# Feed-forward in chunks of 384 tokens instead of 256, with a quarter of the decoded weights kept in DRAM

## The chip, the cores and the metric

One core of a Trainium2 chip runs the whole kernel. The metric is the device time of one execution in microseconds (us). A core has engines that run side by side, each with its own list of instructions: TensorE (PE, matmuls; its weight loads are shown as PEld), VectorE (DVE), ScalarE (ACT), GpSimd (POOL), and SyncE (SP), which here issues every DMA. They wait for each other on semaphores. Matmuls write PSUM, eight banks of 128 x 512 fp32; everything else lives in SBUF.

## What is computed

Attention over 8 batches, 8 heads, 576 tokens and 64 wide heads, as the sum of a pooled part (means of 4 tokens, full attention, repeated 4 times) and a local part (keys less than 4 tokens away); then a layer norm without bias, a feed-forward block with ReLU, and a residual. `moe_w_ch1` is 512 x 2048 and `moe_w_ch2` 2048 x 512, both float64, and the kernel reads them as pairs of 32-bit words.

```python
x = transpose(out_up + out_local).reshape(8, 576, 512)
mu = np.mean(x, axis=-1, keepdims=True)
var = np.mean((x - mu) ** 2, axis=-1, keepdims=True)
xn = (x - mu) / np.sqrt(var + 1e-06) * g_ln
ch = np.maximum(xn @ w_ch1, 0.0) @ w_ch2
return (x + ch).astype(np.float32)
```

## The kernel before

**Tiles and chunks.** The 8 x 576 = 4608 tokens are 36 tiles of 128. The feed-forward takes two tiles at a time: 18 chunks of 256 tokens. The 2048 inner units are 16 blocks of 128; the code handles them in 8 pairs.

**Three products for one.** Weights and activations are each split in a high and a low word of fp32r, and a product is high x low + low x high + high x high. The first product ("up", line 996) takes for a block of 128 units 12 matmuls: three terms by four pieces of the 512 inputs, with the weights as the loaded operand and 256 tokens as the moving one. The output `h` (one PSUM bank for the two blocks of a pair) goes through ACT (`hh` = ReLU rounded to fp32r, line 1003) and DVE (`hl` = the remainder, line 1007). The second product ("down", line 1019) takes `hh` and `hl`, 128 tokens by 128 units, as the loaded operand and 512 output columns of `w2` as the moving one, three matmuls a tile and block, and adds up in one PSUM bank `acc` per tile over all 16 blocks. At the end DVE adds the residual `x` (1027) and SP stores it (1033).

**Weights.** Each of the 32 keys (w1 or w2, block f) is loaded as int32 words (`s`, 347 and 352, two DMAs of 256 KB), put together by ACT (359), DVE (367, 370) and ACT (378, the high word `hi`), and DVE or POOL (383, the low word `lo`). All 64 decoded words stay in SBUF to the end.

**Norm.** A tile's `x` is the local part, copied to its rows by DMA from `xl` (659, 662), plus `up`, the pooled part, loaded from DRAM (865) and added by POOL (896). Statistics (904 to 910) and `xn` (914) follow, four transposes on PE (`px`, 923), then ACT writes `xh` (930) and DVE the remainder `xlo` (940), which the up matmuls of the chunk read.

**Rooms.** Nearly all SBUF tiles come from one pool of 88 equal units of 128 x 512 fp32, "u": raw loads, decoded weights, `xh`, `xlo`, `hh`, `hl`, `x`, `xl`, and the rest. An instruction that writes a unit waits until the last reader of what lay there is done, a DMA included.

**The order** is made by the class `Plan` (23 to 136). Every piece of work is a task with an engine, a planned duration, dependencies, a due time, the rooms that it takes and gives back, and for loads how early it may go out (`ahead`). `order()` lays the tasks out in planned time and emits them; each engine then runs its list strictly in that order, SP too. Chunks 0 and 1 are due at the same time and advance with the weights; from chunk 2 on one chunk is due every 53 planned us. Attention tasks of later batches stand between the feed-forward tasks: `ls`, `lt`, `lv` are scores, transposes and products with V of the local part (40 windows), `gq`, `gs`, `gt`, `gv` those of the pooled part.

Of the kernel before, what the change touches and what calls it, by code (L numbers as in the profile page):

```python
# [139 lines left out]
def attention_then_ffn(  # L140
# [131 lines left out]
    C1 = 5  # L272
    CHUNK = 53
    PACE = CHUNK / NPR

    def chunk_at(c):
        return T0 + (C1 * c if c < 2 else CHUNK * c)

    def pair_at(c, p):
        return chunk_at(c) + (2 * PACE if c < 2 else PACE) * p  # L280

    def norm_at(n):
        c, j = divmod(n, TPC)
        return chunk_at(c) - 6.0 + 1.0 * j
# [50 lines left out]
    weight = {}  # L335

    def weights(which, f):
# [42 lines left out]
        def low(eng):  # L380
# [24 lines left out]
    def local(i):  # L405
# [212 lines left out]
        t = add("PE", 0.75, scores_by_pair if by_pe else scores_by_block, turned, due - 6.0,  # L618
# [10 lines left out]
        for h2 in range(2):  # L629
            t = add("DVE", 0.28, lambda h2=h2: inverse(h2), (tv,), due)  # L630
# [20 lines left out]
        for e, (n, p0, r0, m, par) in enumerate(moves):  # L651

            def move(n=n, p0=p0, r0=r0, m=m, par=par):
# [7 lines left out]
                for h2 in range(2):  # L661
# [5 lines left out]
            t = add("SP", 0.76 if by_pe else 1.52, move, outs, due + 1.0, take=() if n in piece else U,  # L667
                    give=U if e == len(moves) - 1 else (), lag=LAT, kb=116)
# [58 lines left out]
    def pooled_pair(b, hg, pr, x, ready):  # L727
# [120 lines left out]
        t = add("DVE", 0.68, divided, (t,), due, take=U if b < NPB and pr == 0 else (), give=A)  # L848
# [7 lines left out]
    def norm(n):  # L856
        add = plan.add
        c, j = divmod(n, TPC)
# [66 lines left out]
        def split_hi(i):  # L925
            if j == 0:
                xh.setdefault(c, []).append(unit([P, 2, T], f"xh{c}_{i}", F32R, "xh"))
            for k in range(2):
                kc = 2 * i + k
                nc.scalar.activation(  # L930
                    xh[c][i][:, k, j * P : (j + 1) * P], pxt[n][:, kc], AF.Copy, scale=gain[:, kc : kc + 1]
                )

        def split_lo(i):
            if j == 0:
                xlo.setdefault(c, []).append(unit([P, 2, T], f"xlo{c}_{i}", F32R, "xlo"))
            ts = slice(j * P, (j + 1) * P)
            for k in range(2):
                kc = 2 * i + k
                nc.vector.scalar_tensor_tensor(  # L940
                    out=xlo[c][i][:, k, ts], in0=pxt[n][:, kc], scalar=gain[:, kc : kc + 1],
                    in1=xh[c][i][:, k, ts].bitcast(F32), op0=ALU.mult, op1=ALU.subtract,
                )

# [23 lines left out]
        t = add("DVE", 0.46, normed, (t, kept) if by_pe else (t,), due, take=U, ahead=12.0, give=A if by_pe else ())  # L968
        t = add("PE", 0.43, turn, (t,), due + 1.0, take=A, give=U, ahead=6.0)
        hi, lo = [], []  # L970
        for i in range(2):
            hi.append(add("ACT", 0.52, lambda i=i: split_hi(i), [t] + hi + his.get(c, []), due + 1.5,
                          take=() if j else rooms("xh")))
        for i in range(2):
            lo.append(add("DVE", 0.53, lambda i=i: split_lo(i), [hi[i]] + lo + xt_done.get(c, []), due + 1.5,
                          take=() if j else rooms("xlo"), give=A if i else ()))
# [4 lines left out]
    hh, hl, acc, ph = {}, {}, {}, {}  # L981
    f2_done, f1_last = {}, {}

    def ffn(c, p):
        add = plan.add
        due = pair_at(c, p)

        def up(fi):
            if fi == 0:
                ph[c, p] = psa(f"h{c}_{p}").rearrange("p (f t) -> p f t", f=2)  # L990
            f = 2 * p + fi
            wh, wl = (w.rearrange("p (c f) -> p c f", c=KC) for w in weight[1, f])
            n = 0
            for wt, xx in ((wl, xh[c]), (wh, xh[c]), (wh, xlo[c])):
                for kc in range(KC):
                    nc.tensor.matmul(  # L996
                        ph[c, p][:, fi], lhsT=wt[:, kc], rhs=xx[kc // 2][:, kc % 2], start=n == 0, stop=n == 3 * KC - 1
                    )
                    n += 1

        def relu():
            hh[c, p] = unit([P, 2, T], f"hh{c}_{p}", F32R, "hh")
            nc.scalar.activation(hh[c, p], ph[c, p], AF.Relu)  # L1003

        def rest():
            hl[c, p] = unit([P, 2, T], f"hl{c}_{p}", F32R, "hl")
            nc.vector.scalar_tensor_tensor(  # L1007
                out=hl[c, p].rearrange("p c t -> p (c t)"), in0=ph[c, p].rearrange("p c t -> p (c t)"), scalar=0.0,
# [107 lines left out]
```

## Time and profile before

| | |
|---|---|
| three runs | 1078.21, 1080.64, 1084.43 us; median 1080.64 |
| span of the profiled execution | 1080.9 us (no other time of it is recorded) |
| granted TensorE clock, mean | 0.989 |
| instructions | 23774; DMA issues 1165, all by SP |
| HBM | 82.58 MB read, 11.80 MB written |
| DMA queue share of 16 engines | 40.2% |

The page of the profile has, in this order: busy time of each engine; the span in 40 slices; DMA queues; the chain of work that ended last, with its shares by engine and by line; the costliest groups of instructions (line, engine, operation, output<-inputs, shape, count, busy time, mean duration, and the idle time of the engine just before them with what ended it); and the DMA issues. Other views are made from the same trace: PE's waits, stretches of time ("windows"), and the timeline, whose rows are start, duration, engine, line, operation, output<-input, shape, count, and in brackets the idle time before it and what ended that.

Two things about these numbers. Matmuls overlap in the array, so a row's duration is longer than the distance to the next start. And what a wait of one engine costs depends on whether another engine waits behind it.

### The profile page before, as it was taken

The page shows a single profiled execution, that of the slowest core. Times are in us where ns is not written, and L with a number is a line of the kernel's source. Part 1 is how long each engine was busy: PE and PEld are TensorE (multiplying, and loading weights), DVE is VectorE, ACT ScalarE, POOL GpSimd, SP SyncE. Part 2 cuts the span into 40 slices and gives each one's busy share as a digit, 9 for nine tenths or more (in the row PEclk, how much of TensorE's full clock was granted, in tenths as well). Part 3 has the DMA queues.
Part 4 walks back from the last instruction along what each step waited for, and adds up shares of the span by engine and source line. Part 5 has one row for each costly group of instructions (what it writes and reads, how often), then busy time and mean ns, then how long its engine had stood idle before and what let it go on. Part 6 is the DMA issues. An engine that isn't in the chain of part 4 may idle for free.

```text
span 1080.9 us, 23774 instructions
## 1 busy us (share of the span) xinstructions
PE 1040.3 (96%) x9290; PEld 933.6 (86%) x9290; DVE 511.9 (47%) x1309; ACT 312.7 (29%) x852; POOL 266.2 (25%) x285
## 2 busy tenths in 40 slices
PE   8987999989989999999999999999979999999998
PEld 8875898978879898989898989898968988888997
DVE  7699954434243535345344443645424353543211
ACT  5675633222222322132222221223212222222110
POOL 4234454314004221141213231142311400100000
PEclk9999899989999999999999999999999999999999
DMA  7798554625333443344343435252533333300000
GB/s 155 211 270 235 121 147 112 144 61 120 82 88 89 99 97 79 65 92 107 82 110 77 109 69 125 47 137 51 126 87 76 69 74 74 85 10 30 9 20 20
DMA packets 289296, 104.34 MB, mean 97 GB/s; under 512 B 237945, under 2 KB 276089, under 8 KB 289185
## 3 DMA queue, kind: packets, MB, share of 16 engines
q1 hardware_dynamic: 289185, 102.83, 40.2%
q8 instruction: 73, 1.20, 0.5%
q14 instruction: 38, 0.31, 0.1%
HBM read 82.58 MB, written 11.80 MB: 87 GB/s over the span
## 4 chain that ended last, share of the span: by engine, by line
PE 78%; DMA 9%; DVE 5%; SPq 4%; issue 2%; ACT 1%; POOL 1%; DVEq 0%; ACTq 0%; POOLq 0%
PE h L996 33%; PE acc L1019 32%; PE gv L802 3%; DMA s<-in_moe_w_ch_dram 2%; PE lv L596 2%; PE ls L540 2%; DMA x<-xl 2%; PE gs L766 2%; PE lt L575 1%; SPq L419 1%; PE px L923 1%; PE gt L785 1%; SPq L662 1%; DVE cva L370 1%; SPq L428 1%
## 5 line engine op out<-in xcount | busy, mean ns | idle before, releaser
L1019 PE MATMUL acc<-hi,hl 128*128 128x512 f32 x576 | 239.1, 415 | 10.2 <-DVE hl L1007 8.5
L1019 PE MATMUL acc<-lo,hh 128*128 128x512 f32 x576 | 228.5, 397 | 0.0
L1019 PE MATMUL acc<-hi,hh 128*128 128x512 f32 x576 | 226.8, 394 | 0.0
L1007 DVE SCALAR_TENSOR_TENSOR hl<-h,hh 128x512 fp32r<-128x512 f32 x144 | 98.9, 687 | 242.8 <-ACT hh L1003 222.8
L1003 ACT ACTIVATE hh<-h 128x512 fp32r<-128x512 f32 x144 | 86.1, 598 | 433.5 <-PE h L996 379.7
L996 PE MATMUL h<-xh,lo 128*128 128x256 f32 x1152 | 193.5, 290 | 0.0
L996 PE MATMUL h<-xlo,hi 128*128 128x256 f32 x1152 | 185.6, 284 | 0.0
L996 PE MATMUL h<-xh,hi 128*128 128x256 f32 x1152 | 185.6, 283 | 0.0
L996 PEld LDWEIGHTS h<-xh,lo 128*128 128x128 f32 x1152 | 169.4, 190 | 17.6 <-POOL lo L383 0.2
L996 PEld LDWEIGHTS h<-xlo,hi 128*128 128x128 f32 x1152 | 159.4, 192 | 0.0
L996 PEld LDWEIGHTS h<-xh,hi 128*128 128x128 f32 x1152 | 159.1, 192 | 0.0
L896 POOL TENSOR_TENSOR x<-x,up 128x512 f32<-128x512 f32 x32 | 41.2, 1289 | 376.8 <-DMA x<-xl 264.5
L1019 PEld LDWEIGHTS acc<-hi,hl 128*128 128x128 f32 x576 | 110.1, 191 | 27.5 <-DVE hl L1007 11.4
L1019 PEld LDWEIGHTS acc<-hi,hh 128*128 128x128 f32 x576 | 109.2, 190 | 25.3
L1019 PEld LDWEIGHTS acc<-lo,hh 128*128 128x128 f32 x576 | 110.3, 191 | 12.7
L930 ACT ACTIVATE xh<-px,gain 128x128 fp32r<-128x128 f32 x144 | 44.3, 367 | 79.5 <-PE px L923 43.6
L940 DVE SCALAR_TENSOR_TENSOR xlo<-px,gain,xh 128x128 fp32r<-128x128 f32 x144 | 43.0, 344 | 38.3 <-ACT xh L930 26.1
L904 DVE BATCH_NORM_STATS2 st<-x 128x6 f32<-128x512 f32 x32 | 22.1, 690 | 69.9 <-POOL x L896 68.7
L1027 DVE SCALAR_TENSOR_TENSOR x<-acc,x 128x512 f32<-128x512 f32 x36 | 24.3, 683 | 35.5 <-PE acc L1019 35.3
L546 DVE TENSOR_TENSOR ls<-ls,mask 128x256 f32<-128x256 f32 x66 | 27.0, 424 | 27.3 <-PE ls L540 22.3
L779 ACT ACTIVATE ag<-gs,gmx 96x144 f32<-96x144 f32 x96 | 28.8, 373 | 35.1 <-DVE gmx L771 33.1
L802 PEld LDWEIGHTS gv<-vd,agt 72*72 72x72 f32 x512 | 37.1, 145 | 1.5
(195 smaller groups left out, 1152.7 us busy)
## 6 DMA issues: line engine op xcount, KB each, us to landing
s<-in_moe_w_ch_dram SPq DMA_DIRECT2D x64, 256.0 KB
vwin<-in_v_dram SPq DMA_DIRECT2D x160, 64.0 KB
out_dram<-x SPq DMA_DIRECT2D x36, 256.0 KB
qr<-in_q_dram SPq DMA_DIRECT2D x264, 32.0 KB
kr<-in_k_dram SPq DMA_DIRECT2D x264, 32.0 KB
up<-ud SPq DMA_DIRECT2D x28, 256.0 KB
x<-xl SPq DMA_DIRECT2D x66, 58.0 KB
ud<-od SPq DMA_DIRECT2D x32, 72.0 KB
```

The costliest lines, as they stand in the source:

```text
L546: nc.vector.tensor_add(x.ps[n], x.ps[n], mask.unsqueeze(1).broadcast_to([P, NPAIR, 64]))
L779: nc.scalar.activation(y.a[:, c], y.ps[:, c], AF.Exp, scale=POOLED_SCALE, bias=y.mx[:, c : c + 1])
L802: nc.tensor.matmul(y.pv[:, qh, h2], lhsT=y.at[kh][:, h2, qh * GH : (qh + 1) * GH], rhs=vd[:, kh, 2 * pr + h2], start=kh == 0, stop=kh == 1,)
L896: nc.gpsimd.tensor_add(xt[n], xt[n], x.up)
L904: nc.vector.bn_stats(st, x.up if by_pe else xt[n])
L930: nc.scalar.activation(xh[c][i][:, k, j * P : (j + 1) * P], pxt[n][:, kc], AF.Copy, scale=gain[:, kc : kc + 1])
L940: nc.vector.scalar_tensor_tensor(out=xlo[c][i][:, k, ts], in0=pxt[n][:, kc], scalar=gain[:, kc : kc + 1], in1=xh[c][i][:, k, ts].bitcast(F ...
L996: nc.tensor.matmul(ph[c, p][:, fi], lhsT=wt[:, kc], rhs=xx[kc // 2][:, kc % 2], start=n == 0, stop=n == 3 * KC - 1)
L1003: nc.scalar.activation(hh[c, p], ph[c, p], AF.Relu)
L1007: nc.vector.scalar_tensor_tensor(out=hl[c, p].rearrange("p c t -> p (c t)"), in0=ph[c, p].rearrange("p c t -> p (c t)"), scalar=0.0, in1=h ...
L1019: nc.tensor.matmul(acc[c][j], lhsT=lt[:, fi, ts], rhs=rt, start=p == 0 and fi == 0 and n == 0, stop=p == NPR - 1 and fi == 1 and n == 2,)
L1027: nc.vector.scalar_tensor_tensor(out=x, in0=acc[c][j], scalar=1.0 + 2.0**-23, in1=x, op0=ALU.mult, op1=ALU.add)
```

## The change

- **Chunks.** The tiles are dealt out as 4, ten times 3, and 2: 12 chunks. Chunk 0 has 512 tokens and handles them as two parts of 256 columns; chunks 1 to 10 have 384 tokens and their up matmuls 384 columns; chunk 11 has 256.
- **Blocks one at a time.** `h` holds one block of up to 512 tokens instead of two blocks of 256. ReLU and remainder work on 128 x 384.
- **Rooms.** 88 units become 73. `xh` and `xlo` of chunks 1 to 11 get 4 buffers of their own ("xx"), high and low word of the hidden activation 2 ("hx").
- **A quarter of the weights.** For blocks 3, 7, 11 and 15 the decoded words are written to DRAM after decoding (`keep`) and their units given back after chunk 0. Every later chunk loads them anew (`again`): 4 blocks, two weights, two words, 256 KB each. Such a load may be issued up to 9 planned us before it is due, and is due 5 us before its block.
- **Plan.** Due times by tile (26 planned us each) instead of by chunk; some planned durations and lags are raised (for the DMAs from `xl` a lag of 4.0 in place of 2.5), which changes the order alone.

The core of the diff:

```diff
-    T = 256
     NT = B * S
     NTILE = NT // P
-    TPC = T // P
-    NCH = NT // T
+    TILES = [4] + [3] * ((NTILE - 4) // 3)
+    TILES += [NTILE - sum(TILES)] if sum(TILES) < NTILE else []
...
+    T = 3 * P
-    NPR = DFF // T
+    NF = DFF // P
+    KEPT = (3, 7, 11, 15)
-    NU, NSTG = 88, 2
+    NU, NSTG, NX, NHX = 73, 2, 4, 2
...
+        def keep():
+            stored[key] = dram.tile([2, P, 512], F32, tag=f"w{name}", bufs=1, name=f"w{name}")
+            for i in range(2):
+                nc.sync.dma_start(stored[key][i], weight[key][i].bitcast(F32))
...
+        if f in KEPT:
+            kept_done[key] = add("SP", 2 * DMA, keep, (t,), due + 6.0, lag=LAT, kb=512)
+        return t
+
+    def again(which, f, c, due):
+        key = (which, f)
+
+        def load():
+            words = [unit([P, 512], f"w{which}_{f}_{c}_{i}") for i in range(2)]
+            for i in range(2):
+                nc.sync.dma_start(words[i], stored[key][i])
+            weight[key] = [t.bitcast(F32R) for t in words]
+
+        return plan.add("SP", 2 * DMA, load, (kept_done[key],), due - 5.0, take=(("u", 2),), lag=LAT, kb=512, ahead=9.0)
...
+            elif j == 0:
+                to[c] = work.tile([P, KC, T], F32R, tag="xx", bufs=NX, name=f"{nm}{c}")
...
-        def up(fi):
+        def up():
+            ph[c, f] = psa(f"h{c}_{f}")
             wh, wl = (w.rearrange("p (c f) -> p c f", c=KC) for w in weight[1, f])
+            terms = [(wt, xx, kc) for wt, xx in ((wl, xh[c]), (wh, xh[c]), (wh, xlo[c])) for kc in range(KC)]
+            for part in range(2 if c == 0 else 1):
+                out = ph[c, f][:, 2 * P * part : 2 * P * (part + 1)] if c == 0 else ph[c, f][:, :tokens]
+                for n, (wt, xx, kc) in enumerate(terms):
+                    rhs = xx[:, kc, :tokens] if c else xx[2 * part + kc // 2][:, kc % 2]
+                    nc.tensor.matmul(out, lhsT=wt[:, kc], rhs=rhs, start=n == 0, stop=n == 3 * KC - 1)
 
         def relu():
-            hh[c, p] = unit([P, 2, T], f"hh{c}_{p}", F32R, "hh")
-            nc.scalar.activation(hh[c, p], ph[c, p], AF.Relu)
+            if c:
+                both = work.tile([P, 2, T], F32R, tag="hx", bufs=NHX, name=f"hx{c}_{f}")
+                hx[c, f] = [both[:, i, :tokens] for i in range(2)]
+            else:
+                hx[c, f] = [unit([P, 512], f"h{n}{c}_{f}", F32R) for n in "hl"]
+            nc.scalar.activation(hx[c, f][0], ph[c, f][:, :tokens], AF.Relu)
...
+        wide = 0.00044 * tokens if c and tokens > 2 * P else 0.12 * n_t / 2
+        t = f1_last[c] = add(
+            "PE", 12 * wide, up, xt_done[c] + [w[0], f1_last.get(c)], due, take=A,
...
```

How it moves the instructions, at three places. First PE in the steady part: a block's up matmuls followed by down matmuls. Before (rows are line, operation, output<-inputs, output shape, and x for repeats; `xh`, `xlo` are the words of the normed tokens, `hi`, `lo` those of a weight, the last number is the tile's):

```order
L996 MATMUL h_2_3637<-xh_0_3371,lo_5_1437 128x256 x2
L996 MATMUL h_2_3637<-xh_1_3404,lo_5_1437 128x256 x2
L996 MATMUL h_2_3637<-xh_0_3371,hi_5_1424 128x256 x2
L996 MATMUL h_2_3637<-xh_1_3404,hi_5_1424 128x256 x2
L996 MATMUL h_2_3637<-xlo_0_3394,hi_5_1424 128x256 x2
L996 MATMUL h_2_3637<-xlo_1_3429,hi_5_1424 128x256 x2
L1019 MATMUL acc_0_3683<-hi_0_1186,hl_0_3597 128x512
L1019 MATMUL acc_0_3683<-lo_0_1211,hh_0_3578 128x512
L1019 MATMUL acc_0_3683<-hi_0_1186,hh_0_3578 128x512
L1019 MATMUL acc_1_3684<-hi_0_1186,hl_0_3597 128x512
L1019 MATMUL acc_1_3684<-lo_0_1211,hh_0_3578 128x512
L1019 MATMUL acc_1_3684<-hi_0_1186,hh_0_3578 128x512
```

PE with the change, a block in chunk 1 whose w1 was loaded again (`w_3_1`):

```order
L1037 MATMUL h_3_3150<-xh_2807,w_3_1_1_3071 128x384 x4
L1037 MATMUL h_3_3150<-xh_2807,w_3_1_0_3070 128x384 x4
L1037 MATMUL h_3_3150<-xlo_2808,w_3_1_0_3070 128x384 x4
L1061 MATMUL acc_0_3088<-hi_2_1462,hx_2_3130 128x512
L1061 MATMUL acc_0_3088<-lo_2_1484,hx_2_3130 128x512
L1061 MATMUL acc_0_3088<-hi_2_1462,hx_2_3130 128x512
L1061 MATMUL acc_1_3089<-hi_2_1462,hx_2_3130 128x512
L1061 MATMUL acc_1_3089<-lo_2_1484,hx_2_3130 128x512
L1061 MATMUL acc_1_3089<-hi_2_1462,hx_2_3130 128x512
L1061 MATMUL acc_2_3090<-hi_2_1462,hx_2_3130 128x512
L1061 MATMUL acc_2_3090<-lo_2_1484,hx_2_3130 128x512
L1061 MATMUL acc_2_3090<-hi_2_1462,hx_2_3130 128x512
```

Twelve up matmuls now serve three tiles instead of two, and the down matmuls of a block come as nine.

Second, SP in the front, where the last two loads of w2 stand (`s_14`, `s_15`; `raw` are loads for pooling, `ud` is the pooled result on its way to DRAM). Before:

```order
L700 DMA raw3q_2133<-in_q_dram 72x4x256
L825 DMA ud_2093<-od_1_2121 72x2x128
L700 DMA raw3k_2148<-in_k_dram 72x4x256
L352 DMA s_14_0_2156<-in_moe_w_ch_dram 128x512
L352 DMA s_14_1_2157<-in_moe_w_ch_dram 128x512
L700 DMA raw3v_2187<-in_v_dram 72x4x256
L700 DMA raw3v_2204<-in_v_dram 72x4x256
L352 DMA s_15_0_2222<-in_moe_w_ch_dram 128x512
L352 DMA s_15_1_2223<-in_moe_w_ch_dram 128x512
```

SP with the change:

```order
L892 DMA up_2604<-ud_1966 128x1x512
L726 DMA raw5k_2640<-in_k_dram 72x4x256
L688 DMA x_1464<-xl_2588 58x4x64 x2
L688 DMA x_1464<-xl_2588 30x4x64 x2
L688 DMA x_2663<-xl_2588 28x4x64 x2
L359 DMA s_14_0_2712<-in_moe_w_ch_dram 128x512
L359 DMA s_14_1_2713<-in_moe_w_ch_dram 128x512
L892 DMA up_2752<-ud_1966 128x1x512
L851 DMA ud_2755<-od_0_2738 72x2x128
L359 DMA s_15_0_2762<-in_moe_w_ch_dram 128x512
L359 DMA s_15_1_2763<-in_moe_w_ch_dram 128x512
```

The loads have moved behind those of the pooled keys of the fifth half batch and behind the first moves of the local part into `x`: the load for block 15 was SP's 174th transfer and is its 235th.

Third, ACT around the `xh` of one tile and the tile after it, with the semaphores that an instruction waits for (`PE`, `DVE`, `Activation` are engines, `DMAHW0` to `DMAHW7` the DMAs). Before, tiles 26 and 27, the place at 800 to 810 us of the trace:

```order
L1003 ACTIVATE hh_5_10352<-h_5_10287 128x512 [waits PE_49]
L1003 ACTIVATE hh_6_10402<-h_6_10355 128x512 [waits PE_49]
L930 ACTIVATE xh_0_10420<-px_10404,gain 128x128 [waits PE_49,Activation_49]
L930 ACTIVATE xh_0_10420<-px_10404,gain 128x128
L930 ACTIVATE xh_1_10438<-px_10404,gain 128x128 [waits DMAHW4_49,DMAHW5_49,DMAHW1_49,DMAHW6_49,DMAHW0_49,DMAHW7_49,DVE_49,Activation_49]
L930 ACTIVATE xh_1_10438<-px_10404,gain 128x128
L930 ACTIVATE xh_0_10420<-px_10468,gain 128x128 [waits PE_49]
L930 ACTIVATE xh_0_10420<-px_10468,gain 128x128
L1003 ACTIVATE hh_7_10494<-h_7_10425 128x512 [waits DMAHW2_49,DVE_49]
```

ACT with the change, two tiles of a later chunk:

```order
L1045 ACTIVATE hx_12_6825<-h_12_6798 128x384 [waits PE_49,Activation_49]
L955 ACTIVATE xh_6870<-px_6849,gain 128x128 [waits PE_49]
L955 ACTIVATE xh_6870<-px_6849,gain 128x128
L955 ACTIVATE xh_6870<-px_6849,gain 128x128 [waits DVE_49]
L955 ACTIVATE xh_6870<-px_6849,gain 128x128
L1045 ACTIVATE hx_13_6918<-h_13_6827 128x384 [waits PE_49,Activation_49]
L955 ACTIVATE xh_6870<-px_6895,gain 128x128 [waits PE_49]
L955 ACTIVATE xh_6870<-px_6895,gain 128x128
L955 ACTIVATE xh_6870<-px_6895,gain 128x128 [waits DVE_49]
L955 ACTIVATE xh_6870<-px_6895,gain 128x128
```

`xh` and the hidden activation no longer wait for DMAs there: in the whole list of ACT 13 of 136 rows of `xh` and 46 of 144 of `hh` named a DMA before, with the change none of 128 and 2 of 192.

More of the change, by code (lines that the diff above doesn't have):

```diff
@@ L847, in pooled_pair @@
         lastg.v = lastg.vd[hg] = t
-        t = add("DVE", 0.68, divided, (t,), due, take=U if b < NPB and pr == 0 else (), give=A)
+        t = add("DVE", 0.8, divided, (t,), due, take=U if b < NPB and pr == 0 else (), give=A)
         od_done.append(t)
@@ new lines, in rest, with down @@
+                op0=ALU.max, op1=ALU.subtract,
+            )
+        def down():
+            if f == 0:
+                acc[c] = [psa(f"acc{c}_{j}") for j in range(n_t)]
+            wh, wl = weight[2, f]
+            hh, hl = hx[c, f]
+            for j in range(n_t):
+                ts = slice(j * P, (j + 1) * P)
+                for n, (lt, rt) in enumerate(((hl, wh), (hh, wl), (hh, wh))):
+                    nc.tensor.matmul(acc[c][j], lhsT=lt[:, ts], rhs=rt, start=f == 0 and n == 0, stop=last and n == 2)
@@ L1042, in ffn @@
-        f1_last[c] = ups[-1]
-        t = add("ACT", act(512), relu, ups, due, take=rooms("hh"))
-        t = add("DVE", dve(512), rest, (t,), due, take=rooms("hl"), give=A)
-        prev = f2_done.get(c)
-        for fi in range(2):
-            prev = add(
-                "PE", 1.38, lambda fi=fi: down(fi), (t, wdone[2, 2 * p + fi], prev),
-                due + (2 * PACE if c < 2 else PACE) * (OFF0 if c < 2 else 2) + 0.1 * fi,
-                take=(("a", TPC),) if p == 0 and fi == 0 else (), give=rooms("hh", "hl") if fi else (),
-            )
@@ L1052, in ffn @@
-        f2_done[c] = prev
-        if p == NPR - 1:
-            for j in range(TPC):
-                t = add("DVE", dve(512), lambda j=j: finish(j), (prev,), due + 1.5 * PACE, give=A)
-                add("SP", DMA, lambda j=j: store(j), (t,), due + 2 * PACE, give=U, lag=LAT + 0.7, kb=256)
-    plan.add("POOL", 2.5, make_masks, (), 0.0)
-    choice_done = plan.add("POOL", 4.0, make_choice, (), 10.0, take=U)
+        fresh = c and f in KEPT
+        lag = step(c) * (OFF0 if c == 0 else OFF)
+        w = [again(i, f, c, due + (lag if i == 2 else 0.0)) if fresh else wdone[i, f] for i in (1, 2)]
@@ L1061, in attention_then_ffn @@
+        if last:
+            for j in range(n_t):
+                t = add("DVE", dve(512), lambda j=j: finish(j), (prev,), due + 1.5 * step(c), give=A)
+                add("SP", DMA, lambda j=j: store(j), (t,), due + 2 * step(c), give=U, lag=LAT + 0.7, kb=256)
+    plan.add("POOL", 4.3, make_masks, (), 0.0)
+    choice_done = plan.add("POOL", 7.3, make_choice, (), 10.0, take=U)
     spread_done = plan.add("POOL", 2.5, make_spread, (choice_done,), 20.0, take=U)
```

146 lines of the change are left out of this document (70 added, 76 removed).

## The prediction

> **What bounds the kernel now.** I read the page's busy shares and its chain of waits first, then the groups, then single rows of the timeline.
>
> ```profile
> span 1080.9 us, 23774 instructions
> PE 1040.3 (96%) x9290; PEld 933.6 (86%) x9290; DVE 511.9 (47%) x1309; ACT 312.7 (29%) x852; POOL 266.2 (25%) x285
> PE 78%; DMA 9%; DVE 5%; SPq 4%; issue 2%; ACT 1%; POOL 1%; DVEq 0%; ACTq 0%; POOLq 0%
> ...
> L996 PE MATMUL h<-xlo,hi 128*128 128x256 f32 x1152 | 185.6, 284 | 0.0
> ...
> L1019 PE MATMUL acc<-hi,hh 128*128 128x512 f32 x576 | 226.8, 394 | 0.0
> ```
>
> TensorE (PE) carries 78% of the chain; the other engines have room. The two feed-forward lines are the largest groups, but their mean durations overlap and cannot be added. The price of one matmul is the distance between starts, and that stands in the timeline:
>
> ```profile
> 902.72 0.64 PE L996 MATMUL h<-xlo,hi 128*128 128x256 f32 x4
> ...
> 903.40 0.60 ACT L1003 ACTIVATE hh<-h 128x512 fp32r<-128x512 f32 x1
> ...
> 904.03 0.69 DVE L1007 SCALAR_TENSOR_TENSOR hl<-h,hh 128x512 fp32r<-128x512 f32 x1 [1.70 <-ACT hh L1003]
> ...
> 907.24 0.64 PE L996 MATMUL h<-xh,lo 128*128 128x256 f32 x4
> ...
> 908.19 0.64 PE L996 MATMUL h<-xlo,hi 128*128 128x256 f32 x4
> ...
> 911.18 0.40 PE L1019 MATMUL acc<-hi,hl 128*128 128x512 f32 x1
> ...
> 911.87 0.40 PE L1019 MATMUL acc<-hi,hl 128*128 128x512 f32 x1
> ```
>
> Between 907.24 and 908.19 eight up matmuls of 256 columns start: 0.1188 us each. Between 911.18 and 911.87 three down matmuls of 512 columns start: 0.230 us each. One block of 128 inner units for 256 tokens is 12 of the first and 6 of the second, 1.43 + 1.38 = 2.81 us. Sixteen blocks in 18 chunks make 808 us of the span. The rest is attention on PE, a front in which weights are decoded, and waits. PE's waits from 160 us to 1060 us, and four stretches (columns: stretch and length; busy PE, PEld, DVE, ACT, POOL; granted clock; DMA share; GB/s):
>
> ```profile
> PE px L923 <- DVE xn L914: 12.7, 5, 5.8
> PE lt L575 <- ACT la L570: 5.0, 1, 5.0
> ```
>
> ```profile
> 60.00:140.00 80.00, 66.38 (x507) 58.70 (x507) 73.36 (x136) 46.92 (x123) 32.94 (x27) 0.94 0.72 193
> 80.00:100.00 20.00, 13.53 (x131) 10.81 (x132) 19.51 (x32) 11.36 (x30) 10.60 (x9) 1.00 0.96 280
> 200.00:1000.00 800.00, 782.33 (x7065) 702.24 (x7065) 346.84 (x916) 197.32 (x540) 178.99 (x184) 0.99 0.38 85
> 800.00:900.00 100.00, 93.01 (x825) 83.60 (x824) 44.92 (x117) 24.06 (x65) 19.35 (x20) 0.97 0.32 73
> ```
>
> So after the front the kernel is PE work plus some 20 us of waits. In the front (60 to 140 us) VectorE (DVE) is busy for 73 of 80 us with decoding, and PE idles for 13.6.
>
> **Term 1, the wider matmul.** Ten chunks of 384 tokens have 160 blocks of 12 up matmuls: 1920 matmuls of 384 columns instead of 2880 of 256. The first and the last chunk keep 256 columns, and the down matmuls stay 1728 of 512 columns, in another order. Nothing else in PE's list changes in number. No row shows 384 columns. By columns alone one would cost 1.5 x 0.1188 = 0.1782 us: no gain. At the rate per column of the 512-column shape it is 0.75 x 0.230 = 0.1725; on the line through both shapes 0.1744. The new code's own price, 0.00044 us a column, is 0.169; it is a claim of the planner and I use it only as the far end. I take 0.1725, the nearest wide row: 1920 x 0.0057 = **10.9 us less**; ends 0 and 17.7.
>
> The Trainium skill ("TensorE: Matmul & The Clock Gate", section "Back-to-back issue gap") gives a gap of N/2.4 + 2.5 ns, so 109.2 ns at 256 and 162.5 at 384, and by that the widening would bring 1920 x 1.3 ns = 2.4 us only. The trace doesn't follow it at 256 columns (118.8 ns).
>
> **Term 2, the buffers of xh.** The longest wait of PE, read along its chain:
>
> ```profile
> 795.22 3.14 SPq L437 DMA_DIRECT2D vwin<-in_v_dram  x4
> 798.46 5.99 SPq L662 DMA_DIRECT2D x<-xl  x6
> ```
>
> ```profile
> 801.75 1.29 POOL L896 TENSOR_TENSOR x<-x,up 128x512 f32<-128x512 f32 x1 [26.71 <-DMA x<-xl]
> ...
> 808.30 0.62 ACT L930 ACTIVATE xh<-px,gain 128x128 fp32r<-128x128 f32 x2 [8.93 <-DMA x<-xl]
> 808.96 0.61 DVE L940 SCALAR_TENSOR_TENSOR xlo<-px,gain,xh 128x128 fp32r<-128x128 f32 x2 [4.17 <-ACT xh L930]
> 809.48 0.54 DVE L914 TENSOR_SCALAR xn<-x,mv 128x512 f32<-128x512 f32 x1
> ...
> 810.08 0.47 PE L923 MATMUL px<-ident,xn 128*128 128x128 f32 x1 [5.78 <-DVE xn L914]
> ```
>
> ```profile
> 802.83 5.25 DMA x<-xl
> ```
>
> The tile's residual was summed at 803.0, so data is not what is late. `xh` of the tile before waited 8.93 us for a DMA that reads `xl`, though its inputs are in PSUM: the shared buffer that it writes into was still being read. Its `xlo` stood ahead of `xn` on DVE, and PE waited behind both. The third pair of orders in the section on the change shows this wait on that very instruction; now `xh` has buffers of its own, and none of its 128 rows waits for a DMA. I count the 12.7 us as **gone**, and with the longest of them the dip of the granted clock in 800:900, 3% of 100 us, **3 us**. What is late next: `xn` itself. In the order, the shortest PE work between a window's last product with V and the `px` that needs it grows from 13.1 to 18.8 us, so I leave nothing. Ends: 0 (the same transfer holds up another instruction that shares those buffers) and 15.7. The wait of 5.0 us at `lt` I leave in; if it goes too, 8 us more with the clock.
>
> **Term 3, waits added.** `hx` has two buffers where `hh` and `hl` took any free unit, so relu of block f waits for down of f-2. Behind it ACT holds the copies `agt` and `at`, which PE's `gv` and `lv` need. From the last up matmul (902.72 + 0.64) to the end of `hl` (904.72) it is 1.36 us. In the new order the PE work between an up and its own down is 1.4 us once, 2.3 us three times and 2.8 us fourteen times; before, never under 4.4. One DVE instruction of 0.69 ahead makes the chain 2.05, two make it 2.7. I take **3 us more**; ends 0 and 18 (1 us at each of the 18 places).
>
> **Term 4, storing and loading.** 176 transfers of 256 KB bring the words of blocks 3, 7, 11, 15 into chunks 1 to 11, 46 MB; 16 store them first, 4 MB. Prices from rows of the same size:
>
> ```profile
> L352 SPq DMA_DIRECT2D s<-in_moe_w_ch_dram x32: 327/415/697, 41.6 to 146.8; - x32
> ```
>
> ```profile
> 173.21 3.33 DMA up<-ud
> ```
>
> ```profile
> 69.69 7.39 DMA s<-in_moe_w_ch_dram
> ```
>
> ```profile
> SPq L1033 <- DVE x L1027: 51.9, 15, 35.4
> ```
>
> An issue is 0.42 us, a landing 3.3 us in the steady part and 7.4 in the crowded front: 4.2 to 8.2 us for a pair. SP's queue is in order, so I asked from which PE instruction on a load may start: 30 us of PE work or more lie between it and the use, except in chunk 1 (11.5, 16, 21 us for its first three pairs) and in the last (23). All exceed 8.2: **0**. Bytes: 46 MB in 890 us is 52 GB/s; at the 0.38 for 85 GB/s of 200:1000 the share becomes about 0.61, under the 0.96 of 80:100. What hides them is PE work; without it each pair would cost 4 us or more.
>
> **Term 5, the front.** Chunk 0 has the four tiles that chunks 0 and 1 had, so DVE's decoding and its relu remainders are the same. The order moves the last loads: words of w2 of block 15 are issued as transfer 235, not 174 (second pair of orders), and 11.0 us of PE work, not 43.9, separate the instruction they wait for from their use. The chain behind the load:
>
> ```profile
> L370 DVE SCALAR_TENSOR_TENSOR cva<-s,cva 128x256 int32<-128x256 int32 x64 | 36.6, 612 | 1.1
> ...
> L359 ACT ACTIVATE cva<-s 128x256 f32<-128x256 f32 x64 | 24.3, 436 | 7.8 <-DMA s<-in_moe_w_ch_dram 7.7
> ...
> L378 ACT CAST hi<-cva 128x512 fp32r<-128x512 f32 x32 | 19.7, 619 | 26.0 <-DVE cva L370 22.7 <-DVE gr L809 1.9 <-DVE lr L602 1.2
> ...
> L367 DVE TENSOR_SCALAR cva<-cva 128x512 int32<-128x512 int32 x32 | 18.9, 592 | 4.0 <-ACT cva L359 4.0
> ...
> L383 DVE TENSOR_TENSOR lo<-cva,hi 128x512 fp32r<-128x512 f32 x19 | 16.3, 869 | 1.0 <-ACT hi L378 1.0
> ```
>
> Two issues 0.84, landing 3.3 to 7.4, then 0.87 + 0.59 + 1.22 + 0.62 + 0.87 = 4.17: 8.3 to 12.4 us against 11.0. At most 1.4 us shows there. Seen as a queue it can be worse: transfer 174 went out at 146.8 us, 0.84 us a transfer, and 61 more would be 51 us later, against the 33 us of lead that are lost; 15 us is my bound for a late front. It can also gain: PE's 13.6 idle us and the clock of 0.94 in 60:140 (4 us). I take **0**, ends -17 and +15. The mark to compare with: before, the PE list up to the second pair of chunk 2 holds the same work as the new list up to chunk 1, and that pair starts at
>
> ```profile
> 195.53 1.63 PE h L996 x12
> ```
>
> **Sum**, against the profiled execution's span (0.3 us from the median of the runs, inside their spread): 1080.9 - 10.9 - 12.7 - 3.0 + 3.0 = **1057.3 us**.
>
> **Rivals.**
> (a) *Nothing comes of it.* A matmul costs by its columns (0.1782), and the wait that left `px` comes back at relu or at `lt`: 1080.9 - 15.7 + 15.7 = 1081. For it: only two shapes are known. Against: 512 columns cost 1.94 times 256, not twice. (The page of the Trainium skill named in term 1 would put 2.4 us of gain here.)
> (b) *The loads come late, slower.* SP is in order and stood 35.4 us before one store (row above). If a load is issued less than 8.2 us ahead of its use, PE stops. One stop of 4 us in each of 11 chunks is 44: 1057 + 44 = 1101. It decides from the point where SP runs more than 22 us behind PE's order (30 less 8.2). Against: SP's rows are waits for other engines; it is rarely the late one.
> (c) *The front ends late*, +15: 1072.
> (d) *More goes than I count*: 384 columns at 0.169 (6.8 more) and half of the front's loss won back (8.5): 1042; with the wait at `lt` gone too, 1034.
>
> **How the numbers follow.** Forecast 0.45, (a) 0.14, (b) 0.11, (c) 0.14, (d) 0.16. A measurement of this kernel tells about 0.5%, 5.4 us, from no change. Faster by more: the forecast, (d), and 0.11 of (c), 0.72. The same: (a) and 0.03 of (c), 0.17. Slower: (b), 0.11. The range takes (c), most of (a) and (d) in and leaves (b) out: 1036 to 1084. The likeliest case's own range is 1047 to 1068.
>
> **What would show it.** Right: eight starts of `h` 128x384 take 1.38 us; PE's waits at `px` are under 2 us; no wait of PE for `w` over 1 us; the first up of chunk 1 starts near 195 us. Wrong: starts 0.178 apart; PE waiting for DMA `w`, or `acc` for `hx`, for over 10 us in sum; a first up of chunk 1 after 210 us.

## The result and the profile after

The changed kernel takes 1096.87 us (median of 4, 1093.02 to 1099.58) where the kernel before takes 1079.93 (1078.21 to 1084.43): ratio 1.015, 95% interval 1.012 to 1.018. The profiled execution has a span of 1091.3 us, 10.4 more than before; it is the shortest of the four (1093.02 us), so its rows show less than the usual loss. The forecast was 1057.3.

The page's lines that answer to those shown of before, and the shares of the chain of waits:

```profile
span 1091.3 us, 22374 instructions
PE 1041.2 (95%) x8374; PEld 925.8 (85%) x8374; DVE 513.8 (47%) x1340; ACT 332.0 (30%) x964; POOL 267.0 (24%) x286
PE 81%; SPq 5%; DMA 5%; DVE 4%; ACT 2%; issue 2%; POOL 1%; POOLq 0%; DVEq 0%; ACTq 0%
```

The windows of the changed kernel (columns as before: stretch; PE, PEld, DVE, ACT, POOL busy; granted clock; DMA share; GB/s):

```profile
60.00:140.00 80.00, 74.80 (x560) 67.39 (x557) 69.59 (x126) 45.94 (x121) 38.07 (x33) 0.96 0.85 247
...
200.00:1000.00 800.00, 774.26 (x6114) 686.93 (x6113) 343.70 (x939) 206.70 (x605) 180.83 (x185) 0.98 0.56 140
```

From 200 to 1000 us PE idles 25.7 us; before it idled 17.7. The DMA share came out at 0.56 (0.61 was forecast), far from full. PE's waits of the changed kernel from 160 to 1060 us (us in sum, times, longest):

```profile
PE px L950 <- DVE xn L941: 15.2, 2, 10.4
PE acc L1061 <- DVE hx L1048: 9.2, 2, 4.7
...
PE ls L566 <- DVE hx L1048: 2.8, 1, 2.8
```

All seven rows of this view come to 32.3 us. None names the loaded words `w`. The longest wait, at 284 us, read back in the timeline of the changed kernel: first VectorE and SyncE's queue, then what follows.

```profile
L845 DVE TENSOR_TENSOR od<-gv,gr x1: 421/421/421, 271.4 to 271.4; 72x256 f32<-72x256 f32 x1
```

```profile
270.87 1.03 SPq L415 DMA_DIRECT2D w<-w  x2
271.99 3.20 SPq L445 DMA_DIRECT2D qr<-in_q_dram  x4
275.29 1.47 SPq L726 DMA_DIRECT2D raw6v<-in_v_dram  x1
276.85 3.28 SPq L688 DMA_DIRECT2D x<-xl  x4
280.23 0.94 SPq L851 DMA_DIRECT2D ud<-od  x1
281.23 1.83 SPq L688 DMA_DIRECT2D x<-xl  x2
283.17 1.46 SPq L726 DMA_DIRECT2D raw6v<-in_v_dram  x1
284.72 0.57 SPq L892 DMA_DIRECT2D up<-ud  x1
```

```profile
290.71 1.26 POOL L923 TENSOR_TENSOR x<-x,up 128x512 f32<-128x512 f32 x1
292.00 0.69 DVE L931 BATCH_NORM_STATS2 st<-x 128x6 f32<-128x512 f32 x1 [11.78 <-POOL x L923]
...
293.86 0.52 DVE L1048 SCALAR_TENSOR_TENSOR hx<-h,hx 128x384 fp32r<-128x384 f32 x1
294.31 0.53 DVE L941 TENSOR_SCALAR xn<-x,mv 128x512 f32<-128x512 f32 x1
...
294.89 1.11 PE L950 MATMUL px<-ident,xn 128*128 128x128 f32 x4 [10.37 <-DVE xn L941]
```

The pooled result `od` is there at 271.8, and SyncE (SP) sends it to DRAM at 280.2: 8.4 us in which SP mostly issues one transfer after the other (its waits from 271 to 285 us come to 2.6). So the load `up` is late, GpSimd's sum with it, and VectorE, in order, stands at the statistics with the relu remainder `hx` and `xn` behind it. The waits that the list calls `hx`, at 543 and 800 us, are the same chain, here at 543 (the bracket behind the sum names another transfer, but `up`, which the sum reads, had been issued only 3.3 us before):

```profile
542.28 0.58 SPq L892 DMA_DIRECT2D up<-ud  x1
...
545.55 1.26 POOL L923 TENSOR_TENSOR x<-x,up 128x512 f32<-128x512 f32 x1 [9.23 <-DMA kr<-in_k_dram]
...
547.86 0.55 DVE L1048 SCALAR_TENSOR_TENSOR hx<-h,hx 128x384 fp32r<-128x384 f32 x1
548.46 0.79 PE L1061 MATMUL acc<-hi,hx 128*128 128x512 f32 x1 [4.67 <-DVE hx L1048]
```

The waits at 284, 543 and 800 us are each followed by a stretch at half clock, the longest one by this:

```profile
287.84:298.08 10.24, 3.19 (x10) 2.71 (x11) 5.07 (x13) 1.25 (x4) 3.75 (x4) 0.50 0.63 151
```

From this came **theory A**: SP's in-order queue is so full that the loads push its other transfers back. Its rivals: **B**, the order leaves three tiles wanted at once too little lead; **C**, the loads' bytes slow other transfers; **D**, SP stands waiting for buffers that PE still reads.

### The profile page after: what moved, and what is told of

Its sections match the earlier page's. It is cut to its first block, busy times and chain, and to the rows that moved or that the text cites. A ratio compares the mean times of both kernels' runs of the same rounds, so it can differ in the third digit from the quotient of the medians.

```text
span 1091.3 us, 22374 instructions
## 1 busy us (share of the span) xinstructions
PE 1041.2 (95%) x8374; PEld 925.8 (85%) x8374; DVE 513.8 (47%) x1340; ACT 332.0 (30%) x964; POOL 267.0 (24%) x286
## 4 chain that ended last, share of the span: by engine, by line
PE 81%; SPq 5%; DMA 5%; DVE 4%; ACT 2%; issue 2%; POOL 1%; POOLq 0%; DVEq 0%; ACTq 0%
PE h L1037 33%; PE acc L1061 33%; PE gv L828 3%; PE lv L622 2%; PE gs L792 2%; SPq L688 2%; PE lt L601 2%; DMA s<-in_moe_w_ch_dram 2%; PE px L950 1%; DMA up<-ud 1%; PE ls L566 1%; PE gt L811 1%; SPq L445 1%; SPq L454 1%; DVE cva L377 1%
## 5 line engine op out<-in xcount | busy, mean ns | idle before, releaser
L1061 PE MATMUL acc<-hi,hx 128*128 128x512 f32 x768 | 268.3, 405 | 9.2 <-DVE hx L1048 9.2
L1048 DVE SCALAR_TENSOR_TENSOR hx<-h,hx 128x384 fp32r<-128x384 f32 (+1 forms) x176 | 95.1, 540 | 291.9 <-ACT hx L1045 291.2
L1045 ACT ACTIVATE hx<-h 128x384 fp32r<-128x384 f32 (+1 forms) x176 | 84.9, 482 | 458.0 <-PE acc L1061 326.8
L1061 PEld LDWEIGHTS acc<-hi,hx 128*128 128x128 f32 x768 | 146.6, 191 | 40.2 <-DVE hx L1048 9.4
L1061 PE MATMUL acc<-lo,hx 128*128 128x512 f32 x384 | 153.8, 400 | 0.0
L1037 PE MATMUL h<-xh,lo 128*128 128x384 f32 (+1 forms) x656 | 140.7, 336 | 0.0
L1037 PE MATMUL h<-xh,hi 128*128 128x384 f32 (+1 forms) x656 | 131.8, 323 | 0.0
L1037 PE MATMUL h<-xlo,hi 128*128 128x384 f32 (+1 forms) x656 | 131.6, 323 | 0.0
L1061 PE MATMUL acc<-w,hx 128*128 128x512 f32 x384 | 98.9, 401 | 0.0
L1061 PEld LDWEIGHTS acc<-lo,hx 128*128 128x128 f32 x384 | 73.4, 191 | 12.4
L931 DVE BATCH_NORM_STATS2 st<-x 128x6 f32<-128x512 f32 x32 | 22.1, 690 | 60.8 <-POOL x L923 60.5
```

What stands on the lines that cost most here:

```text
L931: nc.vector.bn_stats(st, x.up if by_pe else xt[n])
L1037: nc.tensor.matmul(out, lhsT=wt[:, kc], rhs=rhs, start=n == 0, stop=n == 3 * KC - 1)
L1045: nc.scalar.activation(hx[c, f][0], ph[c, f][:, :tokens], AF.Relu)
L1048: nc.vector.scalar_tensor_tensor(out=hx[c, f][1], in0=ph[c, f][:, :tokens], scalar=0.0, in1=hx[c, f][0].bitcast(F32), op0=ALU.max, op1=ALU ...
L1061: nc.tensor.matmul(acc[c][j], lhsT=lt[:, ts], rhs=rt, start=f == 0 and n == 0, stop=last and n == 2)
```

## Experiments on the loads

All of these but the one with two blocks keep the changed kernel's order, so only what is named differs. First without the 176 loads and, in the same way, without the 16 stores; no buffers are taken for the words either:

```diff
             for i in range(2):
-                nc.sync.dma_start(stored[key][i], weight[key][i].bitcast(F32))
+                pass
...
-            words = [unit([P, 512], f"w{which}_{f}_{c}_{i}") for i in range(2)]
+            words = weight[which, f - 1]
             for i in range(2):
-                nc.sync.dma_start(words[i], stored[key][i])
-            weight[key] = [t.bitcast(F32R) for t in words]
+                pass
+            weight[key] = words
```

> The order of the changed kernel is kept, but the 176 loads and the 16 stores of words are not issued; in chunks 1 to 11 the blocks 3, 7, 11 and 15 use the words of the block before them, so the output is not the reference's. Theory A (SyncE's queue is too full: 176 loads of 0.44 us each push the load of `up` back, the sum on GpSimd comes late, VectorE's statistics wait for it in order, and PE stops behind them): PE's waits of 10.4, 4.7, 4.5 and 2.8 us at 284, 543, 800 and 246 us go, with their half-clock stretches, 1060 to 1072 us. Rival B (three tiles are now wanted at once ahead of a chunk, and the order leaves the pooled attention too little lead, whatever SyncE carries): the waits stay, within 6 us of the changed kernel, 1090 to 1097.

1069.79 us, ratio 0.990 (0.987 to 0.993): 27 us less than the changed kernel: that is what loads and stores cost together. PE's waits at 284, 543 and 800 us fall to 2.8, 2.8 and 1.9. B falls as the main cause. A fits, but the run takes the bytes and the buffers away too, so it doesn't rule out C and D. The place shown above, in the kernel without loads:

```profile
264.61 0.42 DVE L845 TENSOR_TENSOR od<-gv,gr 72x256 f32<-72x256 f32 x1
```

```profile
266.49 0.90 SPq L851 DMA_DIRECT2D ud<-od  x1
...
281.08 1.11 PE L950 MATMUL px<-ident,xn 128*128 128x128 f32 x4 [2.83 <-DVE xn L941]
```

SP is 1.5 us behind `od` in place of 8.4, and PE's wait is 2.83 in place of 10.37. The queue can be counted over a stretch. Between the 9th and the 12th `ud` (181 to 280 us in the changed kernel) SP makes the same 114 other transfers in both kernels; it takes 98.8 us with loads and stores and 87.3 without, and the rows of the 18 loads and 4 stores in between add up to 9.7. What of a load costs the time, two more kernels separate; they keep the stores and the buffers. In the first the loads are cut to 8 of 512 columns, in the second they are whole; in both the block before's words are used (the second keeps the line of the transfer as it was):

```diff
-                nc.sync.dma_start(words[i], stored[key][i])
-            weight[key] = [t.bitcast(F32R) for t in words]
+                nc.sync.dma_start(words[i][:, :8], stored[key][i][:, :8])
+            weight[key] = weight[which, f - 1]
```

> The changed kernel, with every load issued from the same place of SyncE's queue but cut to the first 8 of 512 columns, 4 KB in place of 256, and the words of the block before used in place of those loaded, so that no buffer of theirs is held. Theory A (issue slots): 1088 to 1097, with `ud` on SyncE up to 8 us behind `od`. Rival C (bytes) and rival D (SyncE waiting for buffers that TensorE still reads): 1068 to 1076, as without loads.

> The changed kernel with all loads and all their bytes, but the words loaded aren't used (the block before's are), so that no load waits for TensorE to leave a buffer of words. Theory A: 1088 to 1097, as with thin loads. Rival C: thin loads fast, this one slow. Rival D: both fast, 1068 to 1076.

1082.57 (ratio 1.002, 1.000 to 1.004) and 1089.69 (1.008, 1.005 to 1.011). No theory was whole. Each step from 1069.8 up to 1096.9 is known to about 4 us:

- **Issues**: thin loads cost 12.8 us, with the 16 stores and the buffers of the words, which the first kernel lacks as well; no run tells these three apart.
- **Bytes**: whole loads cost 7.1 more. SP's loads of `qr` and `kr` then wait 22.1 us in sum for a `w` transfer to land, 0.2 with thin loads.
- **Use of the words**: another 7.2. SP's loads wait 30.4 us behind PE in the changed kernel (12.8 of them in one wait at 1015 us) and 1.8 with unused words, as theory D has it. That these waits make the 7.2 us is argued.

The two largest of those waits behind PE:

```profile
SPq L415 <- PE h L1037: 14.1, 3, 12.8
...
SPq L415 <- PE px L950: 6.3, 2, 5.7
```

The line of the loads, in the changed kernel and with thin loads (durations ns: min, median, max):

```profile
L415 SPq DMA_DIRECT2D w<-w x176: 319/383/1612, 209.4 to 1016.6; - x176
```

```profile
L415 SPq DMA_DIRECT2D w<-w x176: 344/430/1731, 208.0 to 990.5; - x176
```

A transfer of 4 KB takes about as much of SP as one of 256 KB.

Then the loads on another engine's queue (`nc.scalar.dma_start`, `nc.gpsimd.dma_start`):

> The 176 loads are issued from ScalarE's queue at the same places of the order; all bytes still move. Theory A (issue slots on SyncE): as without loads, 1060 to 1075, unless ScalarE, which waits in order for a free buffer, now holds up relu; that would be seen as PE waits at `acc` behind ACT. Rival C (46 MB of transfers slow the landing of the others): no gain, 1090 or more. Rival B: no gain either.

> The 176 loads are issued from GpSimd's queue, at the same places of the order; all bytes still move. Theory A: SyncE's lag goes as without loads, 1068 to 1080, as far as GpSimd's own waits for a free buffer don't hold up the sum of x and `up`. Rival C (the bytes): 1090 or more with the lag between `od` and its store on SyncE gone, yet `up` landing later.

On ScalarE 1112.51 (1.029, 1.025 to 1.033), on GpSimd 1086.90 (1.005, 1.003 to 1.008), between its two forecasts. On ScalarE the load itself blocks, in the order of its queue:

```profile
520.44 7.49 ACTq L415 DMA_DIRECT2D w<-w  x2
...
527.96 0.27 ACT L774 COPY qbdg<-gq 64x144 f32<-64x144 f32 x1 [8.77 <-DMA x<-xl]
...
528.86 1.76 PE L792 MATMUL gs<-ktg,qbdg 128*96 128x144 f32 x6 [4.94 <-ACT ktg L778]
```

Two issues last 7.49 us, held until a transfer that reads `xl` is done (the bracket names it), and the copies for PE's `gs` stand behind them. The Trainium skill ("Perfetto Trace Analysis", section "DMA Optimizations") says that balancing transfers across the issuing engines may help where descriptor generation is the limit. Here it gave 10 us on GpSimd and took 16 on ScalarE, where the copies stood behind the loads.

On GpSimd the longest wait stays, though SP carries no load there:

```profile
PE px L950 <- DVE xn L941: 13.4, 2, 8.9
```

`ud` still goes out 6.8 us behind `od` at that place, and in the stretch counted above SP's moves `x<-xl` take 23.9 us, waits inside them included, against 16.6 without loads. So SP's issues alone are not the cause at this place; what makes the moves longer was not tried.

Last, half the loads, with resident words in their place (`KEPT = (3, 11)`; the planner makes a new order):

> The changed kernel with two blocks (3 and 11) loaded in each chunk in place of four, so 88 loads, and eight more buffers held by resident words. Theory A: about half of what the kernel without loads gained, 1078 to 1088. Rival: the fewer free buffers hold transfers up as much as the loads did: 1090 to 1100.

1109.52 (1.027, 1.021 to 1.033): PE waits 28.3 us at `px` and 9.7 at `h` for a decoded word. That is above both forecasts. Either the fewer free buffers cost it, or the new order by itself; the run doesn't tell these apart.

## Experiments on the lead and the width

More lead for the pooled attention and `up`, with all loads (`- 9.0` becomes `- 17.0` in `g_base`, the load's `due - 4.0` becomes `due - 12.0`):

> All loads stay; the pooled attention of batches 1 to 7 is planned 8 us earlier and the load of `up` is due 8 us earlier. Theory A and rival B both give PE's long waits behind `up` gone, 1065 to 1078, if lead is all that lacks; if SyncE has no slot left for it, another of its transfers is late instead and the time stays at 1085 to 1097.

1106.00 (1.022, 1.020 to 1.025), above all that was forecast: the waits behind `up` go, and others come:

```profile
PE h L1037 <- ACT la L592: 15.6, 2, 8.0
```

At the longer of the two, at 528 us, ScalarE's `la` stands behind VectorE, which waited 9.82 us for one of SP's moves `x<-xl`: an earlier place in SP's queue made another of its transfers late. Without loads the same idea, applied to the tiles (`8.0` becomes `14.0` in `norm_at`), works:

> The wide kernel without loads, with the three tiles ahead of a chunk planned 6 us earlier (14 in place of 8 us ahead of it). If what makes it slower than the narrow one is that three tiles are wanted at once with too little lead, PE's waits of 2.8, 2.8, 1.9 us at 278, 530, 781 us and of 3.4 and 1.9 at 180 go: 1056 to 1062. Rival: other work is moved behind them and waits in their place: 1066 to 1075.

1064.78 (0.988, 0.983 to 0.992): PE's waits from 160 to 1060 us fall from 13.3 to 5.7, the time by 5.0, between the two forecasts. Then chunks of two tiles, without loads:

```diff
-    TILES = [4] + [3] * ((NTILE - 4) // 3)
+    TILES = [4] + [2] * ((NTILE - 4) // 2)
```

> As the kernel without loads, but after the first chunk of four tiles there are 16 chunks of two tiles (256 columns), still one block of 128 inner units at a time. The prediction's first term: 1920 up matmuls of 384 columns become 2880 of 256, 10.9 us more than without loads, 1078, and up to 1088 since each of 96 more blocks also starts with an up matmul that takes about 0.06 us longer and a down that does. Rival (a matmul costs by its columns): within 5 us of the kernel without loads, 1065 to 1073.

1060.68 (0.980, 0.977 to 0.983): **narrower is 9.1 us faster**, which neither theory had. PE's waits from 160 to 1060 us are 4.6 in place of 13.3. And the 256-column matmul is cheaper here than in the kernel before; this is its timeline:

```profile
461.67 0.63 PE L1037 MATMUL h<-xh,hi 128*128 128x256 f32 x4
462.14 0.63 PE L1037 MATMUL h<-xlo,hi 128*128 128x256 f32 x4
```

Four starts in 0.47 us, 0.1175 each, against 0.1188. Over all blocks at full clock from 205 us on, the last eight starts of a block lie 0.1175 apart here and 0.1197 in the kernel before. The narrow chunks with two blocks loaded (`KEPT = (7, 15)`, buffers cut to fit):

> The changed kernel with chunks of two tiles after the first (buffers of xh, xlo and hx cut to 256 columns, 78 shared buffers in place of 73) and only blocks 7 and 15 loaded for each chunk: 128 loads in place of 176, nothing left out. Theory A with what the narrow kernel without loads showed (1060.7): 128/176 of the 27 us that the loads cost, 1075 to 1083. Rival: with chunks of two tiles the transfers are spread out, SyncE doesn't fall behind, and the loads cost under 8 us: 1061 to 1069.

1084.74 (1.005, 1.003 to 1.008), near the forecast and 24 us over the narrow kernel without loads. The order is a new one, so these 24 us are not the loads' alone: the narrow kernel with all words resident (below) loads nothing and is 14.5 us over it.

## Experiments on the buffers and the plan

The kernel before with buffers apart for `xh`, then for both (`SEP = {"xh": 4}`, `SEP = {"xh": 4, "xlo": 4}`):

> The kernel before, with four of its 88 buffers kept for `xh` alone and nothing else of the change. The prediction's second term: no row of `xh` waits for the transfer that reads `xl`, PE's 12.7 us of waits at `px` go and the longest dip of the clock with them: 1064 to 1068. Rival: the order is made anew and the tile is late through something else: 1075 to 1085.

> The kernel before, with four of its 88 buffers kept for `xh` and four for `xlo`. With `xh` alone apart, the same wait came back one step later: `xlo` on VectorE waited 6.13 us for the transfer that reads `xl`. If the shared buffers are the whole of the prediction's second term, both apart take PE's waits at `px` away: 1064 to 1070. Rival: the tile is then late through its own transfers (`up` and the moves from `xl`) and the time stays at 1075 to 1085.

1080.53 (1.000, 0.998 to 1.002) and 1089.38 (1.007, 1.005 to 1.009), the second above both its forecasts. With `xh` apart, the longest wait reads:

```profile
297.62 0.61 DVE L940 SCALAR_TENSOR_TENSOR xlo<-px,gain,xh 128x128 fp32r<-128x128 f32 x2 [6.13 <-DMA x<-xl]
298.14 0.54 DVE L914 TENSOR_SCALAR xn<-x,mv 128x512 f32<-128x512 f32 x1
...
298.74 1.12 PE L923 MATMUL px<-ident,xn 128*128 128x128 f32 x4 [5.55 <-DVE xn L914]
```

The wait moved on by one instruction. With both apart PE still waits 12.4 us at `px`, seven times. The reverse, the narrow kernel without loads with both back in the shared buffers:

> The narrow kernel without loads, with `xh` and `xlo` of all chunks in the shared buffers again (81 of them, the same room in all) and no buffers of their own. The prediction's second term: PE's waits at `px` behind a transfer that reads `xl` come back, 12.7 us with 3 for the clock: 1073 to 1078. Rival (the waits went through the new order, not through the buffers): 1058 to 1064.

1056.57 (0.978, 0.975 to 0.981), PE's waits 1.5 us, somewhat faster than either forecast: the buffers aren't it. The planner's durations, old ones in the narrow kernel and new ones in the kernel before (this line and ten more):

```diff
-            t = add("SP", 0.76 if by_pe else 1.52, move, outs, due + 1.0, take=() if n in piece else U,
+            t = add("SP", 0.85 if by_pe else 1.7, move, outs, due + 1.0, take=() if n in piece else U,
```

> The narrow kernel without loads, with the planner's durations and the lag of the moves as they were before. If the new durations gave the better order, some of the 20 us between the kernel before and the narrow one come back: 1066 to 1078. Rival (they did little): 1058 to 1064.

> The kernel before, with nothing of the change but the planner's new durations and the lag of 4 us for the moves. If they are what took PE's waits at `px` away, 1068 to 1074 and those waits under 5 us. Rival (they help only the order by single blocks): 1076 to 1085.

1066.68 (0.987, 0.984 to 0.990), 6.0 more than with the new ones; and 1072.94 (0.993, 0.990 to 0.995), 8 us less than before, PE's waits at `px` 3.6 in place of 12.7. That is half of what the second term promised, through longer planned durations. `ud` is up to 9 us behind `od` there, so this lag by itself doesn't make a kernel slow. Now nothing left out, all words resident, narrow, shared buffers (`KEPT = ()`, `NU = 86`), and then the same with 16 buffers given back:

> Chunks of two tiles after the first, all words resident, nothing loaded again, `xh` and `xlo` in the shared buffers (86, beside two of `hx` with 256 columns): the room of the kernel before, in the order by single blocks with the new durations; nothing is left out. If that order and the durations made the narrow kernel without loads fast, 1055 to 1064, and it beats both kernels. Rival: the buffers that the loads set free did it (16 in the kernels without loads), and without them it is back at 1070 to 1080.

> The narrow kernel with resident words (1075.2), except that blocks 3, 7, 11 and 15 are decoded but their two words are given back at once, and the block before's are used, so that 16 more of the 86 buffers are free and nothing is loaded again. If the free buffers are what counts, 1053 to 1062. Rival (the order without the planned loads is the worse one): 1070 to 1078.

1075.20 (0.995, 0.993 to 0.996) and 1078.10 (0.998, 0.995 to 1.000). So the good order of the narrow kernels without loads came neither from single blocks nor from free buffers. One thing they share is left to try: their plan reserved SP time for loads that never ran. That slack in the resident kernel, with no load at all:

```diff
-        opts = {eng: (dur, fn, 0.0)}
+        dur *= 1.18 if eng == "SP" else 1.0; opts = {eng: (dur, fn, 0.0)}
```

> The narrow kernel with resident words (1075.2), with nothing changed but the planner's durations on SyncE, all 1.18 times as long: as much of SyncE's time reserved as by the empty loads. If the slack on SyncE is what made that order good, 1054 to 1064, with `ud` issued at most 5 us behind `od`, and nothing left out of the computation. Rival (another order, as good or bad by chance): 1068 to 1082.

**1058.56 us** (1057.78 to 1060.29), ratio 0.979 (0.977 to 0.981): it beats both kernels and leaves nothing out. PE's line and clock on its page:

```profile
PE 1039.2 (98%) x9356; PEld 931.0 (88%) x9356; DVE 522.5 (49%) x1419; ACT 347.5 (33%) x1052; POOL 266.0 (25%) x285
...
PEclk9999999999999999999999999999999999999999
```

PE's waits from 160 to 1060 us, with resident words, and with the plan padded as well:

```profile
PE px L950 <- DVE xn L941: 4.7, 3, 2.0
...
```

```profile
PE px L950 <- DVE xn L941: 1.1, 1, 1.1
PE gv L828 <- DVE hx L1048: 0.5, 1, 0.5
```

All rows come to 10.1 and 1.9 us. `ud` is at most 4.9 us behind `od` in batches 1 to 7, as forecast; with resident words alone it is up to 8.1. Part of the gain lies in the front: with resident words alone the clock stands at half for 13.7 us between 94 and 126 us, and with the padded plan not once before the last 4 us.

## Why the prediction was wrong, step by step

**Term 4 is the step that failed**: stores and loads at 0. Together they cost 27 us, counted on one and the same order. The step asked whether a load comes late for PE, and in the changed kernel it never does. It didn't ask who stands behind a load in SP's queue. Rival (b) put the stop at the loaded words and its threshold at SP 22 us behind PE's order; the place was `up` and the ud store, where a lag of 8 us was enough in this order. "It is rarely the late one" was read off SP's waits for other engines. The signs named for being wrong had none for this path, and none of them came: eight starts of `h` take 1.38 us, PE waits 9.2 us at `acc` for `hx`, not over 10, and the first up of chunk 1 comes before 210 us. A count of SP's work would have raised the question: its rows add up to 702 us in the trace of before and 767 after (each row's duration, waits inside it included), 76 and 81 of the 100 us from 300 to 400.

**Term 1, the wider matmul**, was right where no attention work stands just ahead of a block:

```profile
204.40 0.86 PE L1037 MATMUL h<-xh,lo 128*128 128x384 f32 x4
205.09 0.86 PE L1037 MATMUL h<-xh,hi 128*128 128x384 f32 x4
205.78 0.51 PE L1037 MATMUL h<-xlo,hi 128*128 128x384 f32 x2
```

Eight starts in 1.38 us, as forecast: 0.1725. For the whole kernel the gain was put too high. The first four starts of a wide block that follows attention work lie 0.197 apart, and 107 of the 157 blocks measured follow such work, against 88 of 250 before (blocks of twelve starts at full clock, from 205 us on). The mean over them is 0.1791 us a wide matmul and 0.1221 one of before, so each saves 1.5 x 0.1221 - 0.1791 = 0.0041 us, 7.8 in all and not 10.9. Against the narrow kernel's 0.1209 it is 4.3; and the chunk of three tiles, which it needs, costs more in waits, so that wide is 9.1 us slower net.

**Term 2, the buffers of `xh`**, fell. The waits at `px` came to 15.2 us, not under 2. The row of `xh` waiting for `x<-xl` was real, but a link, not the cause: taken away, `xlo` waited in the same place. Plans with longer durations took most of these waits away with the buffers shared.

**Term 3**: PE's waits behind `hx` came to 12.6 us where 3 were taken, inside the bound of 18, but by another mechanism: VectorE stood at the statistics of a late tile. With the same two buffers they are 4.7 without loads and 0.5 at `gv` in the padded plan.

**Term 5, the front**, at 0, was 7 us: the first up of chunk 1 starts at 202.2, not near 195. From 60 to 140 us PE is even busy 8.4 us more than before; it stops ahead of chunk 1, and the place reads like the one at 284 us:

```profile
171.96 7.61 SPq L688 DMA_DIRECT2D x<-xl  x6
...
180.74 0.59 SPq L892 DMA_DIRECT2D up<-ud  x1
...
186.75 0.71 PEld L950 LDWEIGHTS px<-ident,xn 128*128 128x128 f32 x4 [5.21 <-DVE xn L941]
...
202.22 0.95 PE L1037 MATMUL h<-xh,lo 128*128 128x384 f32 x4
```

It isn't the loads: without them the last sum of chunk 0 starts only 1.9 us earlier. With chunks of two tiles it starts 7.8 us earlier still.

**The sum**: without loads and stores the span is 1066.8, 9.5 over the forecast. The first up of chunk 1 starts at 200.3 there, 4.8 us after the mark of 195.5. From there to the end the kernel before takes 885.4 us and this one 866.5, 18.9 less, where terms 1 to 3 promised 23.6; 3.1 of the 4.7 that lack are the wide matmul's, the rest stays open. Loads and stores add 24.5 in spans, 1.9 ahead of the mark and 22.6 behind it.

Argued, not tried: that the padded plan would do as much for the order before, and how much of its 16.6 us is the slack and how much a lucky order; one factor was run, and it met its forecast. Orders made anew for other reasons moved the time too: up by 3 us (more room), 6 (old durations), 8 (both buffers apart) and 13 (two blocks), down by 5 (more lead for the tiles) and 8 (new durations in the kernel before).

## What to carry to other kernels

A load that is never waited for can still cost time: look at what stands behind it in the issuing engine's queue, and at who waits for that. The queue's busy share alone doesn't tell: SP's rows cover 76 of the 100 us from 300 to 400 in the kernel before, 81 in the changed one, and 77 in the padded one, which is the fastest of the three. Where a planner sets the order, try some slack in the plan for the engine whose lateness spreads before adding work or buffers. Test a suspected buffer wait by taking the buffer away on its own; if the wait moves to the next instruction, the cause stands further up.

## What was not expected of the hardware

An issue on SP costs about the same for 4 KB and 256 KB (430 and 383 ns, rows above). The clock went to half after each PE wait of 2.8 us or more from 200 us on in these runs, for 3.4, 6.8 or 10.2 us, so a wait of 4.7 costs more than 4.7. Some shorter waits brought it too (1.55 us at 583 us with resident words), others not (2.77 us at 301 us in the kernel before). The Trainium skill ("TensorE: Matmul & The Clock Gate", section "What's actually happening") gives a free-running activity window of 3.4 us, and the stretches agree as its multiples. An up block that follows attention work starts with a longer gap, here in the kernel without loads:

```profile
460.62 0.69 PE L566 MATMUL ls<-lkt,lqt 64*64 64x64 f32 x32
...
461.25 0.96 PE L1037 MATMUL h<-xh,lo 128*128 128x384 f32 x4
462.04 0.86 PE L1037 MATMUL h<-xh,hi 128*128 128x384 f32 x4
462.73 0.51 PE L1037 MATMUL h<-xlo,hi 128*128 128x384 f32 x2
```

Four starts take 0.79 us and then 0.69, 0.1 us for the change of work. Why 256 columns cost less with `xh` and `xlo` in buffers of their own (0.1175) than in the shared ones (0.1197 before, 0.1193 in the padded kernel) wasn't tried.
